# Batch 0 of a cross-attention and snake MLP kernel: x loaded flat, attention in token halves, and a new order of all steps

## The chip, the cores and the metric

One NeuronCore of one Trainium2 chip. The metric is device time in microseconds (us); of the kernel before there are three runs, 221.13, 221.16 and 221.43, median 221.16. All durations come from one profiled execution of 221.2 us. Engines: TensorE (PE; its weight loads PEld overlap the products), VectorE (DVE), ScalarE (ACT), GpSimd (POOL) and SyncE (SP, which only issues DMAs). "Landing" is when a DMA signals that its data is there.

## The reference

```python
B, H, S, Ns, D = 8, 8, 512, 32, 64          # x: [B,H,S,D], state: [B,H,Ns,D]
scores = x @ state.T / 8 ; a = softmax(scores)        # over 32 states
xread = a @ state                                     # [B,H,512,64]
scores2 = state @ x.T / 8 ; a2 = softmax(scores2)     # over 512 tokens
sread = a2 @ x                                        # [B,H,32,64]
y = concat([xread, sread], tokens) -> [B*544, H*D=512]
h = y @ w_in                                          # w_in 512 x 2048
s = sin(alpha * h) ; g = h + s*s / (alpha + 1e-9)
out = g @ w_out                                       # w_out 2048 x 512, out [4352, 512] float32
```

## The kernel before

All products are in bf16 with float32 sums in PSUM. `w_in` is folded into the state first: for each batch, `m(b, s)` computes M = state @ w_in for a quarter s of the 2048 columns (eight 64x32 products of 512 columns in both halves g of the heads, which run packed in the array), and `me` evicts it. Then h needs only the normalised attention A, transposed to AT: `h(t, f)` (or `hg`, one product per g) makes a tile of 128 columns of d_ff by 512 tokens with two products, M stationary, AT moving. There are 16 tiles f per batch. `si` applies Sin on ScalarE, `sq` squares it on VectorE (V), ScalarE (A) or GpSimd (G), `gt` adds h on VectorE and frees the PSUM bank of h. `o(t, st, f0, f1)` multiplies gT by w_out for one of four groups st of 128 tokens, 16 products of 512 columns in all; `oc` evicts it, `os` stores it from SP.

Attention of a batch: `sc` scores (128 tokens by 64 states of two heads, per product), `ex` Exp, `rs` row sums, `rr` reciprocals, `nm` normalises to A, then A is transposed: on TensorE for batch 0 (`at`, `ac` copies it out), by a DMA transpose from SP for the others (`ad`). x comes in as `xnat` (`lx`, a cast load from GpSimd, token rows p, each partition holding four tokens of every head), `pk` reorders it to `xp`, and it is transposed on TensorE for batches 0 and 1 and by a DMA transpose (`td`) from batch 2 on. The other side (sread) uses the same E: `w` = xp stationary times E, `cs` the column sums, `rc` and `xs` the division into `xs_all`; its MLP is tile row t = 8 with tiles of 256 columns.

Order: nothing is scheduled at run time. ORDER is a list of steps written out for the whole kernel, and each engine executes its own instructions in the order of that list; the trailing letter is the engine and the trailing digits are PSUM banks (there are eight, one tile each, so a step that takes a bank waits for the readers of what was in it). `warm_up.n.cols.bank` puts n spare products of zeros into a bank. Loads by GpSimd (`li` a quarter of w_in, `lo` a quarter of w_out, `l_st` the whole state, `lx` x of a batch) are carried out in the order in which they are issued; from the ninth on, an issue waits for the landing of the eighth before it.

Before, batch 0's x is loaded as float32 by four DMAs from SP (`lq`, L261, 256 KB each, rows of 1 KB), cast and reordered by ScalarE (`xq`, L356), transposed (`xtq`, L361) and copied out (`xc`, L385). The first two batches' state comes by `l_s01`, is transposed (`s01_t`) and put into `stT` block by block (`s01_k`). `touch_x` and `touch` are tiny first reads of x and w_in. The steps st_t and st_c turn the rest of the state round. The order of GpSimd's loads is st, li.0, li.1, li.2, lo.0, lo.1, lx.1, li.3, lo.2, then (after the two `nm` of batch 0) lo.3, lx.2.

Of the kernel before, what the change touches and what calls it, by code (L numbers as in the profile page):

```python
# [33 lines left out]
me.1.1.1.A warm_up.2.128.2 gt.0.2 si.0.0 warm_up.2.128.2 warm_up.2.128.6 warm_up.2.128.3
warm_up.2.128.2 warm_up.2.128.6 me.0.1.0.A gt.0.1 sq.0.0.G m.0.2.3.2 si.0.3 m.1.2.5.6 hg.0.4.0.7
me.0.2.0.V me.0.2.1.A hg.0.4.1 sq.0.3.G hg.0.6.0.4 me.1.2.1.V hg.0.6.1 si.0.4 hg.0.7.0.3 hg.0.11.0.2
me.1.2.0.V si.0.6 hg.0.7.1 sq.0.4.G hg.0.5.0.6 gt.0.0 hg.0.5.1 si.0.7 hg.0.11.1 hg.0.8.0.5 hg.0.8.1
sq.0.6.A gt.0.3 sq.0.7.G o.0.3.0.2.0 si.0.5 gt.0.4 o.0.3.2.3 o.0.0.0.2.1 si.0.11 o.0.0.2.3 gt.0.6
sq.0.5.G o.0.0.3.4 o.0.2.0.1.7 si.0.8 o.0.3.3.5 sq.0.11.A gt.0.7 hg.0.9.0.4 sq.0.8.G o.0.2.1.2
gt.0.5 o.0.2.2.4 hg.0.9.1 gt.0.11 o.0.0.4.5 hg.0.10.0.3 si.0.9 o.0.2.4.5 gt.0.8 o.0.0.5.6 o.0.3.5.6  # L40
sq.0.9.A o.0.3.6.8 pk.1.0.V hg.0.10.1 xt.1.1.6 pk.1.1.V si.0.10 gt.0.9 xt.1.0.2 xc.1.1.0.A sq.0.10.G
o.0.2.5.6 xc.1.1.1.V xc.1.0.0.A o.0.0.6.7 xc.1.0.1.V o.0.0.7.8 o.0.2.6.7 sc.1.1.5 gt.0.10 sc.1.0.4
m.0.3.6.2 ex.1.0 o.0.2.7.8 me.0.3.0.V o.0.1.0.3.3 me.0.3.1.V o.0.1.3.6 hg.0.13.0.6 o.0.1.6.7 ex.1.1
rs.1.0 hg.0.13.1 m.1.3.2.4 si.0.13 o.0.1.7.8 rr.1.0 rs.1.1 nm.1.0.0.4.G o.0.1.8.9 hg.0.12.0.5
o.0.3.8.9 rr.1.1 hg.0.12.1 me.1.3.0.V o.0.0.8.9 nm.1.1.0.4.G o.0.1.9.10 o.0.0.9.10 me.1.3.1.V
si.0.12 o.0.0.10.11 o.0.3.9.11 sq.0.13.G ad.1 hg.0.15.0.2 sq.0.12.A o.0.1.10.12 hg.0.15.1 gt.0.12
o.0.2.8.10 si.0.15 o.0.2.10.11 gt.0.13 o.0.0.11.12 hg.0.14.0.4 sq.0.15.A hg.0.14.1 o.0.3.11.13
si.0.14 gt.0.15 o.0.0.12.13 o.0.1.12.13 o.0.3.13.14 sq.0.14.A pk.2.0.V o.0.1.13.14 pk.2.1.V h.1.2.5
gt.0.14 h.1.4.6 td.2 si.1.2 lx.3.0.1 h.1.0.2 si.1.4 o.0.0.13.15 sq.1.2.V h.1.1.4 si.1.0 gt.1.2
sq.1.4.G o.0.3.14.16 si.1.1 o.0.2.11.13 sq.1.0.A oc.0.3.V h.1.6.5 sq.1.1.G gt.1.4 o.0.2.13.14 os.0.3  # L50
h.1.3.0 si.1.6 gt.1.0 o.0.1.14.16 si.1.3 sq.1.6.G h.1.13.6 gt.1.1 oc.0.1.A o.0.2.14.15 o.0.0.15.16
si.1.13 h.1.15.2 sq.1.3.G gt.1.6 os.0.1 o.0.2.15.16 oc.0.0.A h.1.5.4 sq.1.13.G oc.0.2.V si.1.15
h.1.7.3 os.0.0 gt.1.3 o.1.1.0.1.5 si.1.5 os.0.2 h.1.8.1 sq.1.15.G gt.1.13 o.1.1.1.2 si.1.7
o.1.2.0.2.7 sq.1.5.A o.1.1.2.3 sq.1.7.G h.1.12.0 gt.1.15 si.1.8 h.1.9.6 gt.1.5 o.1.2.2.3 si.1.12
sq.1.8.G o.1.2.3.5 gt.1.7 si.1.9 o.1.1.3.4 h.1.10.2 sq.1.12.A pk.3.1.V h.1.11.4 sq.1.9.G gt.1.8
o.1.2.5.6 si.1.10 o.1.2.6.7 gt.1.12 h.1.14.3 si.1.11 sq.1.10.G o.1.2.7.8 gt.1.9 sc.2.1.1 si.1.14
o.1.1.4.7 sq.1.11.A pk.3.0.V sq.1.14.G o.1.1.7.8 gt.1.10 td.3 o.1.2.8.9 sc.2.0.0 o.1.1.8.9 gt.1.11
o.1.1.9.10 ex.2.0 o.1.3.0.2.6 gt.1.14 o.1.3.2.4 o.1.2.9.10 o.1.3.4.5 o.1.2.10.12 ex.2.1 o.1.2.12.13
rs.2.0 o.1.1.10.11 m.2.2.2.4.3.0 rr.2.0 rs.2.1 o.1.2.13.14 nm.2.0.0.4.G me.2.3.0.A o.1.2.14.15 w.0.1
rr.2.1 me.2.2.1.A me.2.3.1.V o.1.3.5.6 nm.2.1.0.4.G me.2.2.0.A o.1.3.6.7 o.1.2.15.16 cs.0 oc.1.2.A  # L60
m.2.0.3.4.0.2 ad.2 rc.0 o.1.3.7.8 me.2.1.1.A o.1.3.8.9 sc.3.0.7 xs.0.1 me.2.1.0.A o.1.1.11.12 os.1.2
me.2.0.0.V sc.3.1.2 me.2.0.1.A o.1.1.12.13 o.1.3.9.10 xs.0.0 o.1.3.10.11 ex.3.0 o.1.1.13.16 ex.3.1
rs.3.0 o.1.3.11.13 oc.1.1.A o.1.3.13.14 rr.3.0 h.2.0.0 rs.3.1 nm.3.0.0.4.G os.1.1 o.1.3.14.16 si.2.0
rr.3.1 h.2.1.3 oc.1.3.V nm.3.1.0.4.G h.2.2.4 h.2.8.1 os.1.3 h.2.3.7 lx.4.0.1 ad.3 si.2.2 o.1.0.0.3.2
si.2.8 sq.2.0.V o.1.0.3.4 sq.2.2.G gt.2.0 h.2.4.5 si.2.1 o.1.0.4.6 si.2.3 sq.2.8.G o.1.0.6.7 gt.2.2
h.2.9.6 si.2.4 o.2.3.0.1.0 o.1.0.7.8 sq.2.1.G o.1.0.8.9 sq.2.3.A gt.2.8 o.1.0.9.10 h.2.5.4 si.2.9
gt.2.3 o.1.0.10.11 sq.2.4.G o.1.0.11.12 si.2.5 h.2.7.1 gt.2.1 o.1.0.12.13 sq.2.9.A sq.2.5.G
o.1.0.13.14 gt.2.4 o.1.0.14.15 si.2.7 o.1.0.15.16 o.2.0.0.1.7 gt.2.9 o.2.0.1.2 oc.1.0.A h.2.6.3
sq.2.7.G gt.2.5 o.2.3.1.2 os.1.0 o.2.3.2.3 si.2.6 h.2.10.5 pk.4.1.V pk.4.0.V o.2.3.3.4 sq.2.6.A
# [88 lines left out]
class Steps:  # L158
# [505 lines left out]
```

The softmax here doesn't subtract the row's maximum and nothing guards it: scores larger than these inputs give would overflow.

## Time and profile before

| Quantity | us or share |
|---|---|
| median of three runs | 221.16 |
| profiled execution, first to last instruction | 221.2 |
| TensorE busy (spare products among it) | 215.7 |
| ScalarE / VectorE / GpSimd busy | 173.5 / 162.4 / 107.1 |
| first h product | 15.11 |
| first o product | 22.55 |
| last landing of the queued start loads (lx.2) | 34.68 |
| last product ends / last store lands | 218.1 / 220.3 |

In the rows that follow a timeline line gives start and length in us, engine, line, operation, written tile <- read tiles, shapes, count, and in brackets the idle time before it and who ended it. A stage row gives the stretch, its length, and per engine the busy time and the number of instructions. A product of 512 columns is listed with some 0.38 us because its latency is counted; the next one starts 0.216 us later.

The landings of the start loads, by the DMA issues in narrow windows (issue, then landing): st_nat 3.25, 8.93; li.0 3.99, 11.58; li.1 4.74, 14.12; li.2 5.47, 16.72; lo.0 6.20, 19.20; lo.1 6.94, 21.74; lx.1 7.67, 24.40; li.3 8.55, 26.94; lo.2 9.29, 29.49; lo.3 14.23, 32.03; lx.2 15.04, 34.68.

### The profile page before, as it was taken

To read this page: it belongs to the slowest core of one execution; us is meant where nothing else is said; L and a number is where in the kernel's file an instruction comes from. 1 tells how busy PE (TensorE), PEld (TensorE's weight loads), DVE (VectorE), ACT (ScalarE), POOL (GpSimd) and SP (SyncE) were. 2 spreads that over 40 slices of the span, in tenths; PEclk is the share of its full clock that TensorE was granted. 3 is DMA by queue.
4 is the path that set the end of the run, shared out by engine and by line. 5 is a ranking of instruction groups with operands and counts; after the bars stand their busy time and mean duration, and the time that the engine had idled before them with its cause. 6 is when DMAs were issued, how large, how long until landed. Compare 5 with 4: busy or idle time off the path is not lost.

```text
span 221.2 us, 4330 instructions
## 1 busy us (share of the span) xinstructions
PE 215.7 (97%) x1619; PEld 106.0 (48%) x1619; DVE 162.4 (73%) x286; ACT 173.5 (78%) x297; POOL 107.1 (48%) x115
## 2 busy tenths in 40 slices
PE   7999999999999999999999999999999999999994
PEld 3664454444444444444454444445445555665452
DVE  3468986999678979988888778889766988571201
ACT  3589878998899979998996999798857897685111
POOL 6866626595388728934863377363501072121000
PEclk9999999999999999999999999999999999999999
DMA  6999995953549518375325437380220211012042
GB/s 172 198 206 204 205 203 87 174 199 73 119 127 158 96 50 150 44 190 61 81 41 125 126 95 94 108 117 17 47 99 0 98 47 47 0 50 95 1 142 96
DMA packets 38052, 23.48 MB, mean 106 GB/s; under 512 B 20992, under 2 KB 33680, under 8 KB 38032
## 3 DMA queue, kind: packets, MB, share of 16 engines
q0 software_dynamic: 11648, 8.13, 26.1%
q1 hardware_dynamic: 26128, 15.08, 26.1%
q8 instruction: 12, 0.20, 0.4%
q14 instruction: 8, 0.07, 0.1%
q10 hardware_dynamic: 256, 0.01, 0.1%
HBM read 17.44 MB, written 8.91 MB: 119 GB/s over the span
## 4 chain that ended last, share of the span: by engine, by line
PE 93%; ACT 3%; DMA 2%; SPq 0%; issue 0%
PE o_ps L587 54%; PE h_ps L537 22%; PE m_ps L488 4%; PE h_ps L543 3%; PE h_ps L552 3%; DMA x<-in_x_dram 2%; PE s_ps L399 2%; PE warm_ps L303 2%; PE w_ps L450 2%; PE w_ps L461 1%; PE x_ps L361 1%; ACT L226 1%; ACT s L560 1%; ACT M L496 1%; PE x_ps L376 0%; PE st_ps L333 0%
## 5 line engine op out<-in xcount | busy, mean ns | idle before, releaser
L587 PE MATMUL o_ps<-w_out_sb,gT 128*128 128x512 bf16 (+2 forms) x560 | 137.7, 373 | 0.0
L576 DVE SCALAR_TENSOR_TENSOR gT<-s,inva_sb,h_ps 128x512 bf16<-128x512 bf16 (+1 forms) x144 | 96.6, 714 | 18.8 <-POOL s L201 9.6
L201 POOL TENSOR_TENSOR s<-s 128x512 bf16<-128x512 bf16 (+1 forms) x76 | 76.7, 1021 | 65.9 <-ACT s L560 62.4
L560 ACT ACTIVATE s<-h_ps,alpha_sb 128x512 bf16<-128x512 f32 (+1 forms) x144 | 88.8, 671 | 10.5 <-PE h_ps L543 4.3
L587 PEld LDWEIGHTS <-gT 128*128 128x128 bf16 x560 | 52.3, 98 | 60.3 <-issue 5.0
L537 PE MATMUL h_ps<-AT,M 128*128 128x512 bf16 x224 | 60.8, 379 | 0.0
L537 PEld LDWEIGHTS <-M 128*128 128x128 bf16 x224 | 21.7, 98 | 25.9 <-issue 0.4
L569 ACT ACTIVATE s<-s 128x512 bf16<-128x512 bf16 (+1 forms) x53 | 31.4, 595 | 0.8
L201 POOL TENSOR_TENSOR A<-E,rR 128x512 bf16<-128x512 bf16 x16 | 16.6, 1048 | 25.7 <-ACT o_sb L595 12.7
L595 ACT COPY o_sb<-o_ps 128x512 f32<-128x512 f32 (+2 forms) x24 | 13.7, 571 | 16.6 <-PE o_ps L587 16.5
L496 ACT CAST M<-m_ps 128x512 bf16<-128x512 f32 x35 | 18.6, 594 | 8.2 <-PE m_ps L488 8.1
L496 DVE CAST M<-m_ps 128x512 bf16<-128x512 f32 x29 | 18.9, 679 | 2.5 <-PE m_ps L488 2.1
L595 DVE COPY o_sb<-o_ps 128x512 f32<-128x512 f32 x11 | 7.6, 691 | 13.0 <-PE o_ps L587 12.9
L303 PE MATMUL warm_ps<-warm 128*128 128x128 bf16 (+3 forms) x66 | 9.9, 295 | 1.4 <-DVE warm L209 1.2
L410 DVE TENSOR_REDUCE R<-E 128x16 f32<-128x512 bf16 x16 | 10.4, 658 | 1.1 <-ACT E L406 0.9
L201 DVE TENSOR_TENSOR s<-s 128x512 bf16<-128x512 bf16 (+1 forms) x15 | 6.2, 415 | 6.8 <-ACT s L560 6.7
L488 PE MATMUL m_ps<-w_in_sb,stT 64*32 64x512 bf16 x256 | 10.2, 382 | 0.0
L468 DVE RECIPROCAL rC<-w_ps 128x128 f32<-128x128 f32 x8 | 7.6, 948 | 3.2 <-PE w_ps L461 3.2
L406 ACT ACTIVATE E<-s_ps 128x512 bf16<-128x512 f32 x16 | 8.8, 601 | 1.4 <-PE s_ps L399 1.3
L552 PE MATMUL h_ps<-AT,M 128*128 128x512 bf16 x32 | 9.4, 380 | 0.4 <-ACT M L496 0.4
L543 PE MATMUL h_ps<-xs_all,w_in_sb 128*128 128x256 bf16 x64 | 9.1, 273 | 0.0
L560 ACT ACT_TABLE_LOAD x5 | 6.4, 1283 | 2.2 <-PE h_ps L537 1.1
(56 smaller groups left out, 104.3 us busy)
## 6 DMA issues: line engine op xcount, KB each, us to landing
out_dram<-o_sb SPq DMA_DIRECT2D x33, 256.0 KB, 2.3
xnat<-in_x_dram POOLq DMA_DIRECT2D x7, 512.0 KB, 7.7
w_in_sb<-in_moe_w_in_dram POOLq DMA_DIRECT2D x4, 512.0 KB, 10.3
w_out_sb<-in_moe_w_out_dram POOLq DMA_DIRECT2D x4, 512.0 KB, 16.3
x<-in_x_dram SPq DMA_DIRECT2D x4, 256.0 KB, 4.3
st_nat<-in_state_dram POOLq DMA_DIRECT2D x1, 256.0 KB, 5.7
out_dram<-o_sb SPq DMA_DIRECT2D x1, 192.0 KB, 1.9
s<-in_state_dram SPq DMA_DIRECT2D x1, 128.0 KB, 2.1
```

The costliest lines, as they stand in the source:

```text
L201: {"V": k.nc.vector, "G": k.nc.gpsimd}[eng].tensor_tensor(out, a, b, ALU.mult)
L303: k.nc.tensor.matmul(wp[:, :cols], k.warm[:, 0:k.P], k.warm[:, :cols], start=True, stop=True)
L488: k.nc.tensor.matmul(k.t["m", b, s + n, g][o0:o0 + k.Ns, :], k.stT[k.half(r), b * k.G + g, c0:c0 + k.Ns], k.w_in_sb[k.half(r), 2 * g + h, ...
L496: k.copy(eng)(k.t["M", b][:, g, s * k.FW:(s + 1) * k.FW], k.t["m", b, s, g][:])
L537: k.nc.tensor.matmul(hp[:, :n], k.t["M", t][:, g, fs], k.t["AT", t][:, g, :], start=(g == 0), stop=(g == k.G - 1),)
L543: k.nc.tensor.matmul(hp[:, :n], k.w_in_sb[:, q, fs], k.xs_all[:, q].rearrange("p b j -> p (b j)"), start=(q == 0), stop=(q == k.Q - 1),)
L552: k.nc.tensor.matmul(k.t["h", t, f][:], k.t["M", t][:, g, f * k.P:(f + 1) * k.P], k.t["AT", t][:, g, :], start=(g == 0), stop=(g == k.G - 1),)
L560: k.nc.scalar.activation(s[:, :n], k.t["h", t, f][:, :n], ACT.Sin, scale=k.alpha_sb[:, f:f + 1])
L569: k.nc.scalar.activation(s2[:, :n], s[:, :n], ACT.Square)
L576: k.nc.vector.scalar_tensor_tensor(gT[:, :n], k.t["s2", t, f][:, :n], k.inva_sb[:, f:f + 1], k.t["h", t, f][:, :n], ALU.mult, ALU.add,)
L587: k.nc.tensor.matmul(k.t["o", t, st, half][:, cols], k.t["gT", t, f][:, rows], k.w_out_sb[:, f, cols], start=(f == 0), stop=(f == k.FT - 1),)
L595: k.copy(eng)(o_sb[:, cols], k.t["o", t, st, half][:, cols])
```

## The change

Batch 0's x is read in the flat order of memory: partition = head x 16 + block of 32 tokens, and each partition holds 32 tokens in one run of 8 KB. Tokens 0-7 and 8-15 of every block come as float32 from SP (`lf`), tokens 16-31 by one cast load from GpSimd (`lfb`), which is its first. `xn` casts the first two parts; `xth` transposes four pairs of tokens per part on TensorE. A half e of the tokens is two parts, so scores, Exp, sums, reciprocals, `at0` and `ac0` go by halves, and `hh` makes half an h tile (two products of 256 columns). Scores are now one head per product (64 rows, 32 columns), two rows of the array in turn, against `st0T`, a second copy of the state. For `w.0` x in token order is needed: a DMA transpose `td.0` makes it from xT0, and `w` of batch 0 is 32 products of 32 columns. Stores of batch 0 write rows in the new token order.

The order is new up to the middle of batch 1: GpSimd's loads go lfb, li.0, li.1, lx.1, lo.0, li.2, lo.1, st, then (after two nm) li.3, lo.2, later lx.2, lo.3, lx.3; x of batch 1 is transposed before batch 0's o products begin; o runs one f at a time over all four token groups; `ad.1` and `td.2` follow in the list the issue of lo.3 and lx.3; spare products are of 256 to 512 columns. From the batches 2 on, only bank numbers differ, except `td.0` ahead of `td.3`.

```diff
-touch_x l_s01 consts touch lq.0.S ident_ l_alpha lq.1.S zero.0 warm_up.7.512.3 exp_table lq.2.S
-zero.1 identf.V lq.3.S s01_c.G l_st li.0 xq.0.A s01_t.4 li.1 xtq.0.5 warm_up.1.384.3 xq.1.A
...
+l_s01 ident_ touch_x consts lf.0.S touch zero.0 lfb lf.1.S l_alpha identf.V li.0 zero.1 exp_table
+li.1 s01_c.V warm_up.4.512.7 s01_t.0 lx.1.0.1 s01_0.A s01_k.1.V s01_k.0.A lo.0 xn.0.V
+warm_up.2.512.7 xth.0.0.1 li.2 xn.1.A xc.0.0.V lo.1 warm_up.1.512.0 warm_up.1.256.7 xth.0.1.2 l_st
+xth.0.2.3 xc.0.1.A xth.0.3.4 xc.0.2.A sc0.0.5.6 xc.0.3.V al_t.7 ex0.0.0 sc0.1.0.1 al_c ex0.0.1 inva
+ex0.1.0 rs0.0 ex0.1.1 rs0.1 rr0.0 warm_up.1.480.5 m.0.0.2.3 rr0.1 m.1.0.4.7 nm.0.0.0.2.V
+nm.0.1.0.2.G me.0.0.0.A nm.0.0.2.4.V me.0.0.1.A nm.0.1.2.4.G warm_up.5.512.1 at0.0.5 me.1.0.1.V
+m.0.1.6.0 sin_table li.3 at0.1.1 ac0.0.V m.1.1.2.3 ac0.1.V lo.2 hh.0.0.0.7 me.0.1.1.V hh.0.1.0.5
+hh.0.2.0.1 me.0.1.0.A hh.0.0.1 me.1.0.0.V hh.0.1.1 me.1.1.0.A hh.0.3.0.0 hh.0.4.0.6 me.1.1.1.V
+hh.0.2.1 si.0.0 hh.0.5.0.4 hh.0.3.1 pk.1.0.V si.0.1 hh.0.4.1 pk.1.1.V sq.0.0.G hh.0.5.1 si.0.2
+sq.0.1.V si.0.3 xt.1.1.2 gt.0.1 sq.0.2.G si.0.4 xt.1.0.3 gt.0.0 hh.0.6.0.5 xc.1.1.0.A sq.0.3.G
+gt.0.2 hh.0.6.1 xc.1.1.1.A hh.0.7.0.7 hh.0.7.1 xc.1.0.0.V xc.1.0.1.A o.0.0.0.1.1 sq.0.4.G gt.0.3
+sc.1.1.2 si.0.5 o.0.0.1.2 sc.1.0.3 o.0.0.2.3 ex.1.1 o.0.1.0.1.0 sq.0.5.V o.0.1.1.2 gt.0.4 o.0.1.2.3
...
+me.0.2.1.V o.0.2.4.5 o.0.3.4.5 si.0.7 st_t.0.4 rr.1.0 sq.0.6.G rr.1.1 st_t.1.3 sq.0.7.A st_c.0.0.V
+o.0.0.5.6 nm.1.0.0.4.G st_c.0.1.A gt.0.6 o.0.1.5.6 st_c.1.0.A o.0.2.5.6 hh.0.8.0.4 gt.0.7 st_c.1.1.A
...
 def touch_x(k):
-        k.touched_x = k.const.tile([16, k.H], FP32, name="touched_x")
...
+        k.touched_x = k.const.tile([16, 1], FP32, name="touched_x")
+        k.nc.scalar.dma_start(k.touched_x[:].unsqueeze(2), k.flat()[::8, 0:1, 0:1])
-    def lq(k, q, eng):
...
+    def flat(k):
+        return k.x[0].rearrange("h (b j) d -> (h b) j d", j=32)
+    def lf(k, part, eng):
+        k.t["xa", part] = k.const.tile([k.P, 8, k.D], FP32, name=f"xa_{part}")
         {"A": k.nc.scalar, "S": k.nc.sync}[eng].dma_start(
+            k.t["xa", part][:], k.flat()[:, 8 * part:8 * part + 8, :]
+        )
+    def lfb(k):
+        k.nc.gpsimd.dma_start(k.flat_sb()[:, 16:32, :], k.flat()[:, 16:32, :])
+    def xn(k, part, eng):
+        k.copy(eng)(k.flat_sb()[:, 8 * part:8 * part + 8, :], k.t["xa", part][:])
+    def xth(k, b, part, bank):
+        tp = k.t["xth", b, part] = k.ps(bank, [k.P, 4, k.P], BF16, "x_ps")
+        for m in range(4):
+            j = 8 * part + 2 * m
+            k.nc.tensor.transpose(
+                tp[:, m, :], k.flat_sb()[:, j:j + 2, :].rearrange("p j d -> p (j d)"), k.ident[:]
+            )
+    def td(k, b):
+        if b == 0:
+            xp = k.new(0, "xp", k.xppool, [k.P, 2, k.H, 2, k.D], BF16)
+            k.nc.sync.dma_start_transpose(
+                xp[:].rearrange("p e h r d -> p (e h) (r d)"),
+                k.xT0()[:].rearrange("p e h m t -> p (e h m t)"),
+            )
+            return
+    def sc0(k, half, *banks):
+        for r in range(2):
+            sp = k.t["sc0", half, r] = k.ps(banks[r], [k.P, k.H, k.Ns], FP32, "s_ps")
+        for h in range(k.H):
+            for r in range(2):
+                k.nc.tensor.matmul(
+                    k.t["sc0", half, r][:, h, :],
+                    k.xT0()[k.half(r), half, h].rearrange("d m t -> d (m t)"),
+                    k.st0T[k.half(r), h, :],
+                    start=True, stop=True,
+                )
+    def at0(k, half, bank):
+        tp = k.t["at0", half] = k.ps(bank, [k.P, k.G, 2, k.P], BF16, "a_ps")
+        for i in range(2):
+            for g in range(k.G):
+                k.nc.tensor.transpose(tp[:, g, i, :], k.t["A", 0][:, g, 2 * half + i], k.ident[:])
+    def hh(k, t, f, half, *bank):
+        if bank:
+            k.t["h", t, f] = k.ps(bank[0], [k.P, k.S], FP32, "h_ps")
+        c = slice(256 * half, 256 * half + 256)
+        for g in range(k.G):
+            k.nc.tensor.matmul(
+                k.t["h", t, f][:, c], k.t["M", t][:, g, f * k.P:(f + 1) * k.P],
+                k.t["AT", t][:, g, c], start=(g == 0), stop=(g == k.G - 1),
+            )
     def w(k, b, bank):
+        if b == 0:
+            for h in range(k.H):
+                for i in range(k.C):
+                    r, c = h % 2, h % 4 * k.Ns
+                    k.nc.tensor.matmul(
+                        wc[k.half(r), h // 2, r * k.Ns:(r + 1) * k.Ns],
+                        k.t["xp", 0][:, i // 2, h, i % 2, :], E[:, h // 4, i, c:c + k.Ns],
+                        start=(i == 0), stop=(i == k.C - 1),
+                    )
+            return
     def os(k, t, st, half=None):
+        if t == 0:
+            ov = k.out[0:k.S].rearrange("(b e m r) c -> e r m b c", b=16, e=2, m=8)
+            k.nc.sync.dma_start(ov[st // 2, st % 2][:, :, cols], o_sb[:, cols])
```

The functions ex0, rs0, rr0 and ac0 are the old ones on half of the tokens; xc of batch 0 copies a transposed part into xT0; s01_0 copies the transposed state into st0T.

## The prediction

> **What bounds the kernel now.** I read the page first, then TensorE's busy time by stage, its timeline over the first 24 us, and the landing of each load in narrow windows.
>
> ```profile
> PE 215.7 (97%) x1619; PEld 106.0 (48%) x1619; DVE 162.4 (73%) x286; ACT 173.5 (78%) x297; POOL 107.1 (48%) x115
> ...
> PE   7999999999999999999999999999999999999994
> ...
> DMA  6999995953549518375325437380220211012042
> ```
> TensorE is full in all slices but the first and the last; the DMA engines are full only in the first six (33 us). Busy time by stage (columns TensorE, weight loads, VectorE, ScalarE, GpSimd, clock, DMA share, GB/s):
>
> ```profile
> 0.00:10.40 10.40, 8.60 (x52) 4.68 (x53) 3.78 (x13) 5.27 (x9) 7.88 (x16) 1.00 0.85 184
> 10.40:20.00 9.60, 8.95 (x155) 5.66 (x154) 6.90 (x15) 8.06 (x15) 5.28 (x6) 1.00 1.24 206
> 20.00:24.00 4.00, 4.00 (x19) 1.82 (x20) 4.00 (x7) 4.00 (x8) 3.78 (x5) 1.00 1.38 200
> ...
> 36.00:218.10 182.10, 182.10 (x1291) 87.96 (x1289) 137.82 (x236) 146.07 (x252) 84.10 (x85) 1.00 0.42 90
> ```
> From 20.0 on TensorE never waits: 197.9 us of products, the last at 217.88, and 3.3 us of output behind it. What it does before 20.0 is in its timeline:
>
> ```profile
> 1.19 3.17 PE L303 MATMUL warm_ps<-warm 128*128 128x512 bf16 x7 [1.19 <-DVE warm L209]
> ...
> 9.74 1.08 PE L303 MATMUL warm_ps<-warm 128*128 128x128 bf16 x10
> ...
> 15.11 0.39 PE L552 MATMUL h_ps<-AT,M 128*128 128x512 bf16 x1
> 15.89 1.24 PE L552 MATMUL h_ps<-AT,M 128*128 128x512 bf16 x5 [0.39 <-ACT M L496]
> ...
> 19.95 2.76 PE L552 MATMUL h_ps<-AT,M 128*128 128x512 bf16 x12
> 22.55 2.32 PE L587 MATMUL o_ps<-w_out_sb,gT 128*128 128x512 bf16 x10
> ```
> "Busy" there is largely spare products. Useful: 48 transposes, 16 scores, six groups of m, 9 of 32 h products, 8 transposes of A: some 6.3 us at full clock. So 13.7 of 20 us are lost, and only these can be won. Spare products of 512 columns start every 427 ns, of 128 columns every 55 ns after 10.4: the clock doubles at 10.4.
>
> **What the skill says.** "TensorE: Matmul & The Clock Gate", Part 1, has the array at half rate until it was busy for one free-running window of about 3.4 us; the doubling at 10.4 agrees. Its Part 4 says that transposes don't count as busy in the same way; no row here shows it. "TensorEngine Tiling (Array Packing)", Key Properties: a change of tiling mode drains TensorE. This agrees: an o product before or after an m group takes 309 ns to the next start instead of 216, so one m group alone costs 0.42 us. "DMA: Bandwidth & Descriptors", Queues, rings and completion order: each DMA engine goes round its queues, so a transpose from SP does not stand behind GpSimd's loads, it shares with them. Issued alone, and together with a transpose, a load of x lands after
>
> ```profile
> xnat<-in_x_dram POOLq DMA_DIRECT2D x1, 512.0 KB, 5.9
> ```
> ```profile
> xnat<-in_x_dram POOLq DMA_DIRECT2D x1, 512.0 KB, 7.7
> ```
>
> **The change, part by part.** *Loads.* Half of x now goes through GpSimd as its first load (lfb), with the shape of st_nat (4 KB read, 2 KB written per partition), which took 5.7 us. GpSimd is free at 1.31, so 7.0 (6.3 without the loads beside it, 7.6 if they slow it more). Behind st_nat (landed 8.93) the next load came 2.65 later, then one each 2.54. Hence li.0 9.65 (before 11.58), li.1 12.2 (14.12), lx.1 14.85 (24.40), lo.0 17.4 (19.20), li.2 19.9 (16.72), lo.1 22.5 (21.74), st 23.8 (8.93), li.3 26.3, lo.2 28.85, lx.2 31.5, lo.3 34.05 (before: last one 34.68). li.3 and lo.2 now stand behind two nm on GpSimd (issued about 12.4), lx.2 and lo.3 behind four squares (about 19.5): the queue has work until 23.8, so this costs nothing.
>
> *Attention.* s01 lands at 2.86 as before. VectorE casts it (estimate 0.3, from 0.2 to 0.4: no such row), then 8 transposes 0.64, copies 0.36 (ScalarE), 0.43 (VectorE), 0.36 (ScalarE) in turn, cast xn.1 0.62: 5.8. Four groups xth at 0.43 (half clock), the last two held by lfb: 7.07 to 7.93. Scores: 32 instead of 16; the score rows take 29 ns warm, 53 cold, I take 40: to 9.3. Four Exp at 0.36 (the 64x256 copy's time) spaced 0.3: 10.2. Two sums 0.68 and two reciprocals 0.25 on VectorE: 11.45; half of nm 0.33 (estimate from 256 elements of a 512-element sum) and 0.55 on GpSimd (half of 1.05): 11.9. TensorE meanwhile does two m and five spare products (1.1). at0 0.22; VectorE first evicts an m (0.68), then copies AT: **first h product at 13.05**, before 15.11 and then a wait.
>
> New waits, and what stands behind them: on TensorE m.0.1 (needs li.1, 12.2) stands ahead of at0.1 (needs A's second half, 12.4), so a li.1 later than 12.4 holds the second half of every h tile; on VectorE pk.1 (needs lx.1, 14.85) comes up at 15.15, and the square and every gt of batch 0 stand behind it; in before these waited for nothing, since x of batch 1 was read only at 26.9. xn.1 on ScalarE stands behind the state copies, and xth.0.1 behind xn.1. The table loads (1.28 each) are as many as before and the first Sin one comes at 11.8 instead of 13.7.
>
> *VectorE then sets the pace*: ac0.1 0.35, three evictions 0.62, two pk 0.34, a square 0.4, gt.0.1 0.74: 17.1. TensorE has 12 half tiles of h, two products each, 0.218 per half tile (2.62) and the transposes of batch 1 (1.1), at 16.8 it waits for that gt, then for gt.0.0 and gt.0.2 (0.67 each): first o at 18.45 (before 22.55).
>
> *To 36 us.* 48 o at 0.216 (10.35), 8 h (3.49), scores of batch 1 (0.5), st_t (1.1), three single m (1.27) make 16.7; waits 0.95: for xc.1.0.1 on ScalarE (0.3), gt.0.4 (0.2), Exp behind its table load (0.1), the four st_c in a row (0.3). So 36.1. Loads come in time: lo.1 22.5 for 23.4, st 23.8 for 24.3, lo.2 28.85 for 30.05, lo.3 34.05 for 36.1. From there gT and evictions lead the products; I allow 0.1.
>
> *Sum.* Of the 197.9 us that before needs after 20.0, the changed kernel has done by 36.1: 48 o 10.35, 23 h products 4.96, xt 1.1, scores 0.5, one m 0.42, together 17.35. Left 180.5. w.0 becomes 32 products of 32 columns: the trace has 16 at 32 ns (0.51); the skill's floor of 25 ns ("The Clock Gate", Part 1) and this row give 30 ns, 0.96, so +0.5 with the mode change (0 if the two column halves run together, 1.3 if 64-column weights take 55 ns). 36.1 + 180.5 + 0.5 + 0.1 = 217.2 against 217.88: **-0.65 us**. The profiled 221.19 stands 0.03 over the median 221.16, so **220.5**.
>
> *At nothing:* td.0, on SP in front of td.3: 1.75 to 3.2 of issue at about 48, td.3 was issued at 52.2; lands by about 53 and w.0 is at 57. Uncovered, scores of batch 3 would wait. Stores of batch 0 in 8x16 rows: six o_sb buffers hide them. touch_x with 16 elements, moved constants: ScalarE waits for its table anyway.
>
> **The rivals.** *The clock opens late (slower).* In the window that ended at 10.4 the old kernel had 1.75 us of wide spare products; the changed one has 0.4, small scores and transposes, and earlier it stands about 0.7 us at 4.5 waiting for xn.0, 0.3 for lfb. If the window doesn't count as busy, the next ends at 13.8: the five spare products take 2.13 instead of 1.08, at0 ends 13.2, everything behind VectorE comes 1.3 later: 221.8. It decides if TensorE idles over about 0.5 us between 7.0 and 10.4, say li.0 after 10.2. For it: Part 4 and the narrow work; against it: the stretch is filled end to end.
>
> *The lead is lost in the loads (no change).* ad.1 leaves when nm.1.1 ends, now about 27.5 with lo.2, lx.2 and lo.3 still coming (before: 35.02, after the last landing 34.68). It costs a load 1.8 us by the rows above; lo.2 then lands at up to 30.6, lo.3 at 35.9: stalls of 0.6 to 1: 221.1 to 221.5. For it: the margins are 0.5 to 0.9; against: a transpose's own packets are 1.4 us.
>
> *It doesn't do what it says:* half-length h products and the bigger w.0 eat the lead; 1.3 for w.0 gives 221.3.
>
> *More is won:* VectorE's estimates too long, lfb at 6.3: 0.7 to 1.3 earlier, 219.2 to 219.8.
>
> **How the numbers follow.** My ledger 0.45 (219.9 to 220.9; 220.5), late clock 0.22 (221.3 to 222.3), loads 0.13, lead eaten 0.09, more won 0.11. A measurement of this kernel can tell about 0.2% (0.44 us). Faster: 0.11 plus 0.37 of the ledger's 0.45; same: 0.08 of it, 0.06 of loads, 0.06 of eaten; the rest slower. The range leaves 0.1 on each side: 219.2 to 222.2; the ledger's own is 219.9 to 220.9.
>
> **What would show it.** Right: h products start near 13, o near 18.5, TensorE without gaps over 0.3 us after 26, last product near 217.2, scores of 32 columns at 30 to 40 ns. Wrong: spare products still 427 ns apart after 11 (clock); gaps in front of o that end on a w_out load, or a transpose landing over 5 us after issue (loads); w.0 over 1.2 us; lfb after 7.6, which shifts the whole start.

## The result, and the profile after

The changed kernel takes 230.53 us (229.26 to 231.59 in four runs) against 221.21 for the kernel before: a ratio of 1.0406, 95% interval 1.0364 to 1.0447. I had forecast 220.5, faster by 0.3%. The page of one execution of the changed kernel (time 231.59, span 229.6):

```profile
PE 217.3 (95%) x1631; PEld 106.2 (46%) x1631; DVE 167.4 (73%) x291; ACT 173.9 (76%) x299; POOL 104.1 (45%) x112
...
PE   5895999998999979999999999999999999999994
...
PEclk9678899999999999999999999999999999999999
DMA  5999999517837841917715431761040200111042
```

TensorE now has holes in three places where it had none: in slices 1 to 4 (0 to 23 us), of which 2 to 4 also have a clock below 9; in slice 10 (52 to 57 us); and in slice 15 (80 to 86 us). The stages of the start, same columns and stretches as before:

```profile
0.00:10.40 10.40, 7.00 (x74) 3.32 (x82) 4.45 (x15) 5.33 (x11) 6.73 (x14) 0.88 0.86 161
10.40:20.00 9.60, 8.63 (x101) 4.92 (x86) 8.06 (x15) 7.43 (x13) 5.84 (x7) 0.78 1.31 205
20.00:24.00 4.00, 2.33 (x14) 1.53 (x14) 3.80 (x6) 0.97 (x3) 3.30 (x4) 0.69 1.20 206
```

From 20 to 24, where the old kernel was full at full clock (4.00, 1.00), TensorE is busy for 2.33 us at a clock of 0.69 and ScalarE for 0.97, while VectorE works nearly throughout (3.80). TensorE's timeline there, then VectorE's and GpSimd's:

```profile
11.21 2.31 PE L310 MATMUL warm_ps<-warm 128*128 128x512 bf16 x5
...
15.22 2.79 PE L480 MATMUL h_ps<-AT,M 128*128 128x256 bf16 x24
17.95 1.08 PE L385 MATMUL x_ps<-ident,xnat 128*64 128x128 bf16 x32
21.66 1.86 PE L480 MATMUL h_ps<-AT,M 128*128 128x256 bf16 x8 [2.64 <-DVE gT L677]
23.32 0.63 PE L688 MATMUL o_ps<-w_out_sb,gT 128*128 128x512 bf16 x1
```

```profile
17.12 2.45 DVE L355 COPY xp<-xnat 128x1024 bf16<-128x1024 bf16 x2
19.49 1.25 DVE L201 TENSOR_TENSOR s<-s 128x512 bf16<-128x512 bf16 x1
20.86 2.07 DVE L677 SCALAR_TENSOR_TENSOR gT<-s,inva_sb,h_ps 128x512 bf16<-128x512 bf16 x3
```

```profile
17.08 4.57 POOL L201 TENSOR_TENSOR s<-s 128x512 bf16<-128x512 bf16 x4 [2.68 <-ACT s L661]
```

The two pk copies of batch 1 took 1.27 and 1.26 us, the square 1.25. In the same trace the same copies took 0.42 at 38.4 and the same square 0.42 at 24.5. What differs is the last row: GpSimd ran four squares end to end beside them. TensorE waited 2.64 us for the gT behind them.

But a GpSimd square alongside is not enough. In the kernel before, pk.3.1 started inside a row of nine GpSimd squares and still took 0.42 us (GpSimd's square of that moment, then the copy):

```profile
48.45 1.04 POOL L201 TENSOR_TENSOR s<-s 128x512 bf16<-128x512 bf16 x1
49.41 0.42 DVE L348 COPY xp<-xnat 128x1024 bf16<-128x1024 bf16 x1
```

It started 0.08 us before that square ended. In the changed kernel the first copy started 0.05 us after a square of 1.04 us had begun, and the second copy and VectorE's square 0.09 and 0.24 us after the two that followed. One sum fits all three: what was left of the GpSimd square (0.99, 0.98 and 0.98 us) plus 0.28. It fits, to within 0.01 us, every such copy and square in the fifteen profiles that started with more than 0.15 us of a GpSimd product still to run; with less left they took their own 0.42. So the price depends on when VectorE comes, and each of these three had come just after a GpSimd square had started.

The third hole is one wait for the DMA transpose of batch 4's x, which landed 5.9 us after its issue instead of 4.3:

```profile
85.31 0.64 PE L490 MATMUL s_ps<-stT,xT 128*128 128x64 bf16 x16 [1.71 <-DMA xT<-xp]
```

**Three intervals that can be compared.** TensorE's work from the first h product to the first o, from there to the column sums of batch 0 (cs.0), and from there to the last product is the same in all versions of the changed kernel; the third is the same in the kernel before too. Starts of products, in us, from one profile each; the time is the median of four runs (for the second profile of the kernel before, that one execution). The runs of one version lie up to 2.4 us apart, so a difference between two versions whose runs overlap shows little by itself, and the profiled execution can be any of the four: what a change does is read from the intervals.

| Kernel | first h starts | to first o | to cs.0 | to last product | time |
|---|---|---|---|---|---|
| before, first profile | 15.11 | 7.44 | 34.92 | 160.41 | 221.2 |
| before, second profile | 14.02 | 6.66 | 34.92 | 160.43 | 221.2 |
| after | 15.22 | 8.10 | 40.61 | 162.30 | 230.5 |
| pk.1 later | 16.84 | 5.40 | 40.44 | 162.13 | 229.0 |
| two squares to ScalarE | 15.19 | 5.37 | 40.70 | 164.73 | 231.6 |
| start filled | 13.85 | 7.90 | 40.92 | 161.23 | 229.4 |
| pk.1 and pk.3 later | 13.94 | 5.40 | 39.93 | 162.43 | 227.4 |
| the same, narrow spare products | 15.73 | 5.40 | 39.95 | 160.47 | 226.8 |
| the same, batch 4's x early | 16.54 | 5.40 | 39.94 | 160.41 | 227.1 |
| that, start filled | 14.07 | 5.40 | 39.93 | 160.41 | 225.2 |
| that, no contended squares | 14.00 | 5.60 | 39.99 | 160.41 | 225.3 |
| two squares to ScalarE, batch 4's x early | 15.98 | 5.38 | 40.71 | 160.41 | 226.6 |
| after, batch 4's x early | 15.25 | 8.11 | 40.62 | 160.41 | 229.0 |
| squares of VectorE left out | 13.80 | 4.88 | 38.94 | 160.41 | 224.4 |
| squares of GpSimd left out | 13.72 | 5.04 | 39.02 | 160.52 | 223.7 |

### The profile page after: what moved, and what is told of

Read it like the earlier page. It is cut to its first block, busy times and chain, and to the rows that moved or that the text cites. A ratio compares the mean times of both kernels' runs of the same rounds, so it can differ in the third digit from the quotient of the medians.

```text
span 229.6 us, 4360 instructions
## 1 busy us (share of the span) xinstructions
PE 217.3 (95%) x1631; PEld 106.2 (46%) x1631; DVE 167.4 (73%) x291; ACT 173.9 (76%) x299; POOL 104.1 (45%) x112
## 4 chain that ended last, share of the span: by engine, by line
PE 77%; DMA 6%; issue 5%; DVE 5%; POOL 4%; ACT 1%; POOLq 0%; DVEq 0%
PE o_ps L688 45%; PE h_ps L638 18%; PE m_ps L589 4%; DMA w_in_sb<-in_moe_w_in_dram 3%; PE h_ps L644 3%; POOL s L201 3%; DMA xT<-xp 3%; PE s_ps L490 2%; DVE xp L355 2%; DVE gT L677 2%; PE w_ps L551 1%; PE h_ps L480 1%; PE w_ps L562 1%; PE warm_ps L310 1%; DVE M L597 1%
## 5 line engine op out<-in xcount | busy, mean ns | idle before, releaser
L201 POOL TENSOR_TENSOR s<-s 128x512 bf16<-128x512 bf16 (+1 forms) x73 | 73.9, 1026 | 77.3 <-ACT s L661 76.0
L638 PE MATMUL h_ps<-AT,M 128*128 128x512 bf16 x204 | 55.5, 379 | 0.2 <-DVE gT L677 0.2
L638 PEld LDWEIGHTS <-M 128*128 128x128 bf16 x204 | 19.8, 98 | 23.9 <-issue 0.9
L670 ACT ACTIVATE s<-s 128x512 bf16<-128x512 bf16 (+1 forms) x50 | 29.4, 590 | 0.8
L201 POOL TENSOR_TENSOR A<-E,rR 128x512 bf16<-128x512 bf16 (+1 forms) x16 | 16.0, 1014 | 27.1 <-ACT o_sb L696 14.5
L597 DVE CAST M<-m_ps 128x512 bf16<-128x512 f32 x26 | 16.9, 678 | 3.2 <-PE m_ps L589 3.1
L201 DVE TENSOR_TENSOR s<-s 128x512 bf16<-128x512 bf16 (+1 forms) x21 | 10.3, 492 | 8.9 <-ACT s L661 8.6
L589 PE MATMUL m_ps<-w_in_sb,stT 64*32 64x512 bf16 x256 | 11.9, 404 | 0.1
L480 PE MATMUL h_ps<-AT,M 128*128 128x256 bf16 x64 | 8.6, 290 | 2.8 <-DVE gT L677 2.6
L355 DVE COPY xp<-xnat 128x1024 bf16<-128x1024 bf16 x14 | 8.1, 612 | 1.1 <-DMA xnat<-in_x_dram 1.1
L480 PEld LDWEIGHTS <-M 128*128 128x128 bf16 x64 | 6.5, 102 | 4.7 <-issue 3.4
## 6 DMA issues: line engine op xcount, KB each, us to landing
w_out_sb<-in_moe_w_out_dram POOLq DMA_DIRECT2D x4, 512.0 KB, 15.2
```

The source lines that it names most:

```text
L201: {"V": k.nc.vector, "G": k.nc.gpsimd}[eng].tensor_tensor(out, a, b, ALU.mult)
L355: k.copy(eng)(k.t["xp", b][:, :, hs, :], k.t["xnat", b][:, hs, :].rearrange("p h (i d) -> p i h d", i=k.C),)
L480: k.nc.tensor.matmul(k.t["h", t, f][:, c], k.t["M", t][:, g, f * k.P:(f + 1) * k.P], k.t["AT", t][:, g, c], start=(g == 0), stop=(g == k.G ...
L589: k.nc.tensor.matmul(k.t["m", b, s + n, g][o0:o0 + k.Ns, :], k.stT[k.half(r), b * k.G + g, c0:c0 + k.Ns], k.w_in_sb[k.half(r), 2 * g + h, ...
L597: k.copy(eng)(k.t["M", b][:, g, s * k.FW:(s + 1) * k.FW], k.t["m", b, s, g][:])
L638: k.nc.tensor.matmul(hp[:, :n], k.t["M", t][:, g, fs], k.t["AT", t][:, g, :], start=(g == 0), stop=(g == k.G - 1),)
```

## The experiments

**pk of batch 1 moved on VectorE.** It is needed only for w.1.

```diff
-hh.0.3.1 pk.1.0.V si.0.1 hh.0.4.1 pk.1.1.V sq.0.0.G
+hh.0.3.1 si.0.1 hh.0.4.1 sq.0.0.G
...
-o.0.1.3.4 gt.0.5 o.0.2.0.1.6
+o.0.1.3.4 gt.0.5 pk.1.0.V pk.1.1.V o.0.2.0.1.6
```

> The changed kernel with the two pk of batch 1 moved on VectorE from ahead of the first square to behind gt.0.5, where GpSimd has no squares. Theory A (VectorE and GpSimd slow each other: the two copies took 1.27 and 1.26 us beside four GpSimd squares, 0.42 elsewhere, and the square and every gt stand behind them): the two copies return to 0.42 each, TensorE's 2.64 us of waiting ahead of the ninth pair of half products shrinks to under 0.6, first o at about 21 instead of 23.3, and the time falls by 2 to 4 us, to 226 to 228.5. Theory B (VectorE was late because lx.1 landed late and would be late anyway): the wait shrinks by under 1 us, time 229 to 230.5. Theory C (the lead is lost in the half clock, which comes from the narrow work before 8): the wait shrinks, but the time stays at 229 to 230.

229.00 us, 1.5 less than after. VectorE, then TensorE, of this run:

```profile
19.23 0.79 DVE L201 TENSOR_TENSOR s<-s 128x512 bf16<-128x512 bf16 x1 [0.40 <-ACT s L661]
...
25.43 0.75 DVE L355 COPY xp<-xnat 128x1024 bf16<-128x1024 bf16 x2
```

```profile
20.93 1.26 PE L480 MATMUL h_ps<-AT,M 128*128 128x256 bf16 x8 [0.27 <-DVE gT L677]
```

The pair of copies is back at 0.75 us, the wait fell from 2.64 to 0.27, and the first interval from 8.10 to 5.40. The time missed theory A's 226 to 228.5, and 1.5 us is within the scatter of the runs (228.51 to 230.18, against 229.26 to 231.59): this execution's first h started only at 16.84, since lf.1 landed late (the cast behind it began at 8.24 instead of 6.47) and the clock opened only at 16.35 (below). So theory A has the interval; in the time it is not seen.

**Two squares of GpSimd on ScalarE, pk left where it is.** This parts contention from pk's place in the order.

```diff
-pk.1.1.V sq.0.0.G hh.0.5.1
+sq.0.0.A hh.0.4.1 pk.1.1.V hh.0.5.1
...
-si.0.3 xt.1.1.2 gt.0.1 sq.0.2.G si.0.4
+si.0.3 sq.0.2.A xt.1.1.2 gt.0.1 si.0.4
```

> The changed kernel with the squares sq.0.0 and sq.0.2 on ScalarE instead of GpSimd; the two pk of batch 1 stay where they are. Theory A (contention of VectorE with GpSimd): with GpSimd idle from 17 to 19 the pk take 0.42 us each instead of 1.27, the square sq.0.1 about 0.43 instead of 1.26, first o at about 21, time lower by 1.5 to 3.5 us, 227 to 229. If it is only the place of pk in VectorE's order (its own 0.42 each and lx.1's landing), the pk still take about 1.27 and nothing moves: 229 to 231.5.

```profile
17.08 0.75 DVE L355 COPY xp<-xnat 128x1024 bf16<-128x1024 bf16 x2
17.75 0.42 DVE L201 TENSOR_TENSOR s<-s 128x512 bf16<-128x512 bf16 x1
```

Same place, same start as in the changed kernel (17.08 and 17.12), but GpSimd idle: 0.75 instead of 2.45, and the first interval is 5.37. So it is the contention and not the place. The time, however, stayed at 231.57, where theory A had 227 to 229. The gain went later:

```profile
79.78 0.59 PE L638 MATMUL h_ps<-AT,M 128*128 128x512 bf16 x2 [2.29 <-DVE gT L677]
...
85.08 0.64 PE L490 MATMUL s_ps<-stT,xT 128*128 128x64 bf16 x16 [1.68 <-DMA xT<-xp]
```

The load of batch 4's x took 9.9 us here (8.3 in the changed kernel; why it was longer is not shown); VectorE stood at pk.4 with every gt behind it, and then the transpose took 5.9.

**The same with batch 4's x loaded early** (the edit is that of the run named "batch 4's x early" below).

> The kernel with sq.0.0 and sq.0.2 on ScalarE, which gained 2.7 us up to 61 and lost all of it at 77 to 85, now with batch 4's x loaded behind batch 3's, its pk and its transpose ahead of the first squares of batch 2. If the gain was lost only because batch 4's x came late (load 9.9 us, transpose 5.9 us): no wait over 0.5 us between 70 and 90, 227 to 228 instead of 231.6. If something else took it, 229 or more.

226.59 us, 5.0 below and a little better than the 227 to 228 expected; from cs.0 on 160.41 as in the kernel before. The two squares on ScalarE did gain; the late x had taken it.

**TensorE's early waits filled with spare products.**

```diff
-xn.0.V warm_up.2.512.7 xth.0.0.1
+xn.0.V warm_up.7.512.7 xth.0.0.1
...
-warm_up.1.512.0 warm_up.1.256.7 xth.0.1.2
+warm_up.3.512.0 warm_up.1.256.7 xth.0.1.2
```

> The changed kernel with seven instead of two spare products of 512 columns ahead of the first transposes of x and three instead of one ahead of the second ones, so that TensorE's waits of 1.16 and 0.49 us before 7.2 are filled. Theory C (the clock falls back to half between 7.9 and 14.7 since TensorE idled before): full clock from about 4.5 on, the five spare products ahead of at0 take 1.1 instead of 2.3 us, first h product at about 14 instead of 15.2, time lower by 1 to 2 us. Theory A: first h product may come 1 us sooner, but the pk then start no sooner than lx.1 lands (16.3), so the time falls by under 1 us, 229 to 230.5.

The first h is at 13.85, 1.4 us sooner: theory C's size. The time of 229.38, 1.15 less, can't part C from A (the runs, 229.12 to 230.02, overlap the changed kernel's). In the changed kernel the trace has the clock full from 4.5 to 7.9, half to 14.7, full, and half again from 21.5 to 25, after the 2.64 us wait; the five spare products took 2.31. In this run it is full from 7.0 to 20.6, and half again for 3.4 us behind the same wait. In all five profiles with the filled start the clock opens between 6.1 and 7.4 and stays open up to the first h, which comes at 13.72 to 14.07. In the eight without, three open at 4.5 to 4.9 and fall back at 7.9 to 8.3, and five open only at 9.5 to 16.4; their first h is at 13.94 to 16.84 (the two latest, 16.84 and 16.54, also had lf.1 land 1.8 us late). In time it shows further down, where the same filling takes 1.9 us off with ranges that don't touch. The seven products cover TensorE's 1.16 us wait for xn.0; that this wait is what keeps the clock back is the reading that fits, but it was not parted from the sheer amount of work that the fill adds.

**pk.3.1 moved next to pk.3.0**, on top of pk.1's move.

```diff
-sq.1.12.A pk.3.1.V h.1.11.3
+sq.1.12.A h.1.11.3
...
-sq.1.11.A pk.3.0.V sq.1.14.G
+sq.1.11.A pk.3.1.V pk.3.0.V sq.1.14.G
```

> As the run with the pk of batch 1 moved, and pk.3.1 also moved on VectorE from 55.3 (1.26 us beside seven GpSimd squares, TensorE waited 0.75 us behind it ahead of the first scores of batch 2) to just ahead of pk.3.0, after those squares. Theory A: another 0.6 to 1 us lower than that run, and the wait ahead of the scores of batch 2 gone. Rival: the wait belongs to the squares on GpSimd that gt needs, not to pk: under 0.3 us of difference.

227.40, another 1.6, where theory A had 0.6 to 1. The wait of 0.75 us ahead of the scores of batch 2 is gone, but a contended copy remained (53.07, 1.26 us beside GpSimd's last square), so the interval to cs.0 fell by 0.5 only. More than that is not pk.3.1's: the first h of this profile came at 13.94 instead of 16.84, without anything in its edit that could move it.

**Narrow spare products: the same time, 20 products more.**

```diff
-warm_up.2.512.7
+warm_up.7.128.7
...
-warm_up.5.512.1
+warm_up.20.128.1
```

> The kernel with the pk of batches 1 and 3 moved, and in it 7 of the spare products of 512 columns cut into 27 of 128 or fewer in the same time (20 of 128 for 5, and 7 of 128 for 2), nothing else. Theory D (a 16 KB transfer of TensorE's instructions, about every 125 products, runs on one DMA engine for 0.95 us at 78.74, between the last packets of the DMA transpose of batch 4's x at 78.5 and that engine's share of its signal at 79.7, so the transpose lands 1.1 us late and the scores of batch 4 wait about 2.0 us): 20 more products ahead of it bring that transfer some 4 us sooner, before the transpose's packets; the transpose lands about 4.3 us after its issue instead of 6.0, the wait shrinks to about 0.6, and the time falls by 1.0 to 1.6 us, to 225.8 to 226.4. Theory E (the transpose is late only because batch 4's x was loaded late): landing still 5.9 us after issue, time 227 to 227.8.

The DMA rows between issue and landing of batch 4's transpose, of the run before this edit and of this one (queue: packets, MB, share; then the transpose with its time to landing):

```profile
q1 hardware_dynamic: 2080, 0.52, 42.7%
q8 instruction: 1, 0.02, 0.9%
...
xT<-xp SPq DMA_TRANSPOSE x1, 6.0
```

```profile
q1 hardware_dynamic: 2089, 0.54, 56.3%
...
xT<-xp SPq DMA_TRANSPOSE x1, 4.3
```

Such a 16 KB packet on the instruction queue comes about every 125 products of TensorE (91 to 153 in the changed kernel) and takes 0.9 to 1.6 us. The Trainium skill, "Runtime: NRT & Kernel Launch", section Instruction fetch mechanics, has instructions fetched in 16 KiB blocks of 256, a cost "mostly hidden". Size and spacing agree (a product is a weight load and a matmul); what was not hidden here is what the packet did to another transfer. In the changed kernel the data packets of td.4 end and the instruction packet starts at 83.25, it lasts 0.93, and the last two 4-byte packets of the transpose come at 84.17 and 84.18. A landing is sixteen updates of one semaphore: fifteen came from 83.56 to 83.71, the sixteenth at 85.27, and TensorE started at 85.31. The packet accounts for 0.9 us of this; why the last update came 1.1 us behind its packet, where the others took some 0.5, is not shown. In this run the instruction packet came at 75.0, before the transpose, all sixteen updates came from 80.43 to 80.59, and the transpose landed in 4.3 us: cs.0 to last product 160.47 instead of 162.43. Theory D holds for the landing, and it is chance: the position follows from how many products came before. In time the gain was 0.6 at the median, less than the 1.0 to 1.6 expected and within the scatter (225.02 to 227.43), since the clock was at half from 8.3 to 15.2 in this profile (first h at 15.73).

**Batch 4's x loaded behind batch 3's.**

```diff
-lx.3.0.1
+lx.3.0.1 lx.4.0.1
...
-h.2.3.2 lx.4.0.1 ad.3 si.2.2 o.1.0.0.3.0 si.2.8 sq.2.0.V
+h.2.3.2 ad.3 si.2.2 o.1.0.0.3.0 si.2.8 pk.4.1.V pk.4.0.V td.4 sq.2.0.V
...
-si.2.6 h.2.10.6 pk.4.1.V pk.4.0.V o.2.3.3.4
+si.2.6 h.2.10.6 o.2.3.3.4
...
-h.2.11.0 td.4
+h.2.11.0
```

> The kernel with the pk of batches 1 and 3 moved, and batch 4's x loaded right behind batch 3's (about 31.6 instead of 65.5), its pk ahead of the first square of batch 2 and its DMA transpose right behind. Then the scores of batch 4 cannot wait for that transpose, whatever makes it late. Both D and E: the wait of 2.0 us at 78.6 goes, 225 to 226. If the load then disturbs the transposes ad.1 and td.2, waits of over 0.5 us appear at 39 or 52 and the time stays at 226.5 or more.

The tail is 160.41, 2.0 less than with both pk moved alone; ad.1 and td.2 landed in time. The time of 227.1 missed the 225 to 226: its first h started at 16.54, the second-latest start of all: lf.1 was late here too (its cast began at 8.28), and the clock opened at 15.6.

**The same edit alone, on the changed kernel.**

> The changed kernel with that one edit alone: batch 4's x loaded behind batch 3's, pk.4 and td.4 early. Theory D (td.4 lands late behind the transfer of instructions, 2.1 us of wait at 83): 228 to 228.8, about 2 us below the changed kernel's 230.5. If the wait at 83 only moves to the next transposes: 230 to 231.

228.99, 1.5 below the changed kernel, somewhat less than expected and with runs that overlap its own (228.08 to 229.78). The two profiles are the clean comparison: the starts of h and o and cs.0 repeat the changed kernel's to within 0.06 us, and the tail alone is shorter, by 1.89.

**Batch 4's x early and the start filled.**

> As the run with batch 4's x loaded early, and with the seven and three spare products ahead of the first transposes of x. Theory C (clock): full clock before 8 in every run, first h product at 13.3 instead of 13.9, time 0.4 to 1.0 us lower than that run. Rival: after the pk have left, first h waits for li.1 and VectorE's evictions, not for TensorE: within 0.3 us of that run.

225.23 (225.02 to 225.58, against 226.45 to 228.31), 1.9 below, more than theory C's 0.4 to 1.0, and the best of the versions that compute everything. The first h came at 14.07, not 13.3: with the clock open, the loads decide:

```profile
10.51 0.63 PE L589 MATMUL m_ps<-w_in_sb,stT 64*32 64x512 bf16 x16 [0.62 <-DMA w_in_sb<-in_moe_w_in_dram]
...
13.05 0.41 PE L589 MATMUL m_ps<-w_in_sb,stT 64*32 64x512 bf16 x8 [0.51 <-DMA w_in_sb<-in_moe_w_in_dram]
```

**The remaining contended squares on ScalarE, pk.3 behind GpSimd's last square.**

```diff
-sq.0.1.V
+sq.0.1.A
...
-sq.0.10.V
+sq.0.10.A
...
-sq.1.1.V
+sq.1.1.A
...
-sq.1.11.A pk.3.1.V pk.3.0.V sq.1.14.G o.1.1.7.8 gt.1.10 td.3 o.1.2.8.9
+sq.1.11.A sq.1.14.G o.1.1.7.8 gt.1.10 o.1.2.8.9
...
-gt.1.11 o.1.1.9.10
+gt.1.11 pk.3.1.V pk.3.0.V td.3 o.1.1.9.10
```

> As the run with batch 4's x loaded early and the start filled with spare products (225.2), and the three squares that VectorE did beside GpSimd's squares (sq.0.1, sq.0.10, sq.1.1, 0.79 us each instead of 0.42) go to ScalarE (0.63), and both pk.3 with the DMA transpose go behind gt.1.11, after GpSimd's last square. Theory A (what TensorE still loses between 20 and 56, 3.4 us against 0.5 in the kernel before, is the rest of the contention): the waits for gT at 18.2, 42.5 and 55.5 (0.3, 0.2 and 0.3 us) go, 224.2 to 224.8. Theory F (it is the order of o one tile at a time over four token groups, with no gT in store, and the single m): the squares on ScalarE delay the next Sin by as much, 225 to 226.

225.33: nothing. The wait at 56 went, those at 18 and 43 grew from 0.3 to 0.5 and from 0.2 to 0.5. Theory A does not explain what is left.

**Squares left out.** In two versions gT of batches 0 and 1 is made from s where VectorE (8 tiles) or GpSimd (17 tiles) made the square.

```diff
 def sq(k, t, f, eng):
+    if t < 2 and eng == "V":
+        k.t["s2", t, f] = k.t["s", t, f]
+        return
```

> As the run with batch 4's x loaded early and the start filled (225.2), but the eight squares of batches 0 and 1 that VectorE makes are left out (gT is made from s instead of s squared there), so VectorE has some 4.5 us less to do between 16 and 47, and GpSimd's squares no partner to contend with. Theory G (the nine small waits of TensorE between 20 and 56, 2.3 us together, are for a VectorE that has too much to do): at least five of the waits go, 223 to 224. Theory F (they come from the order: o follows each gT at once and only four banks are left for h): the waits stay within 0.6 us in sum, 224.6 to 225.4.

> The same with the seventeen squares of GpSimd in batches 0 and 1 left out instead (gT from s there). Theory H (the waits come through the time of a GpSimd square, 1.04 us, between a Sin and its gT, and through what it costs VectorE): the waits at 18.2, 20.4, 42.5, 47.2, 48.5 and 55.5 go, 1.5 to 2.5 us less, 222.7 to 223.8. Theory F: under 0.6 us less.

224.38 and 223.71: 0.85 and 1.5 less. The first (223.66 to 225.24) overlaps the filled version and lies in neither theory's range. The second (223.53 to 224.12) is clear of it and meets H's range at its upper edge. Of the nine waits that the filled version shows between 18 and 59 us, six go in the first, as G had it, and eight in the second; one new wait comes in each. In the profiles the two save 0.5 and 0.4 before the first o, and 1.0 and 0.9 from there to cs.0. What does that leave? As an estimate I took what TensorE's products of o, h, m, scores and transposes cost at their full rate from the time that passed. Between first o and cs.0 the kernel before loses 0.7 us, the filled version 4.25, these two 3.25 and 3.35. So some 2.6 us of this remain with the squares of one engine gone: in the first version two waits for gT of 0.3, in both the m groups of one quarter (0.37 each around the products), a wait for stT of 0.2, and w.0. That these belong to the order itself (four o banks open from the first f, four left for h and m) is argued, not shown.

**The kernel before again.**

> The kernel before, unchanged, for a second profile: the first profile's span of 221.2 is as long as the median time, while all other runs have a time of 1.9 to 2.0 us over their span. If that first execution was a slow one, this one has a span of about 219.2, and the difference lies before 20 us, in the clock that opened at 10.4 or in waits for the loads of batch 0; if not, the span is 221.2 again.

Its span is 219.3 with a time of 221.24. Two rows of its timeline, to be held against 9.74 (ten products in 1.08) and 22.55 in the first profile:

```profile
10.14 1.62 PE L303 MATMUL warm_ps<-warm 128*128 128x128 bf16 x26
...
20.68 2.32 PE L587 MATMUL o_ps<-w_out_sb,gT 128*128 128x512 bf16 x10
```

The clock opened at 4.15 instead of 10.5, and the first o came 1.87 us sooner; from there on the two profiles are alike to 0.02 us. "TensorE: Matmul & The Clock Gate", Part 1, calls the window free-running and the ramp "run-variable"; two executions of one kernel agree. It calls its cost under 1% of a typical span; here the two differ by 0.8%, which is four times the 0.2% that a measurement of this kernel can tell.

## Why the prediction was wrong

The profiled execution (231.59, the slowest of the four) is 11.1 us over my 220.5. By the intervals: 2.0 of the baseline, 2.2 up to the first h, 2.7 to the first o, 1.9 behind cs.0, and the 2.3 that remain between first o and cs.0.

- **The baseline, 2.0 us: the step "the profiled 221.19 stands 0.03 over the median".** 221.19 was a span. In the runs of the kernel before that state both, the time is 1.85 to 1.94 us more than the span (up to 2.1 in the versions that compute everything, up to 2.5 with VectorE's squares left out), so that execution was some 2 us slower than the median ones. My sum against it gave a span of 220.5, so a time of 222.4: slower, by its own working, before anything else failed. The early hint was in the view that I used: the spare products ahead of 10.4 at half rate, beside a clock column that reads 1.00 there, since the trace's first clock record is only at 10.5.
- **VectorE's chain, 2.7 us: the step "two pk 0.34, a square 0.4".** I took the rate of back-to-back copies from rows where GpSimd was idle, and put the pk next to GpSimd's squares without asking; waiting for GpSimd stood in the sum at nothing. They cost 2.45 and 1.25, which took TensorE's wait from 0.27 to 2.64; another 0.35 of the 2.7 is the half clock that followed that wait. This is the term that failed. The rest of the interval was right: I had 18.45 minus 13.05, 5.40, and with the pk in its place but GpSimd idle it is 5.37. That the five versions with pk.1 moved have exactly 5.40 is in part luck, since there the pk are out of the chain and the square still costs 0.79. The skill has it in "SBUF — State Buffer", section Who interferes with whom: VectorE's copies in a two-port mode, and its products with both inputs in SBUF, share ports with GpSimd, and whoever issues first holds them for its whole instruction. The traces agree with the class (gT and the evictions, which read PSUM, kept their 0.63 to 0.75 us beside GpSimd squares) and with the order: VectorE paid the rest of the square that was running, plus 0.28. In the kernel before the same pair stood side by side for pk.3, and its timing hid it.
- **Up to the first h, 2.2 us.** lf.1 landed at 6.45 where my ledger needs it by about 5, xn.1 ended at 7.1 instead of 5.8, and li.0 and li.1 landed 0.5 late (10.18, 12.72). With the clock open this makes 13.72 to 14.07 instead of 13.05; the rest is the clock, as the rival *the clock opens late* had it: five spare products 2.31 (it said 2.13), at0 begun at 13.32 (it had it ended at 13.2). Its point of decision, idling between 7.0 and 10.4, was wrong by place: TensorE idled 1.16 and 0.49 us before 7.2. The rival also missed that the clock can fall a second time behind a long wait.
- **First o to cs.0, 2.3 us: the steps "waits 0.95" and "gT and evictions lead; I allow 0.1".** 0.5 of it is pk.3.1 beside seven GpSimd squares (this interval is 40.44 with pk.1 moved, 39.93 with pk.3.1 moved as well), the same failing as in the chain. The other 1.8 is only in part explained: the filled version still has four waits for gT of 0.17 to 0.34, 0.97 in all, and leaving out one engine's squares takes 0.9 to 1.0 off the interval. What makes up the rest is open.
- **Behind cs.0, 1.9 us: "from the batches 2 on, only bank numbers differ".** The order was the same and the time was not: the instruction transfer fell on td.4. No step of mine could have priced it; that td.4 had only 0.14 us to spare in the old kernel (landed 76.83, scores at 76.97) was readable.
- **w.0, overpriced:** it costs 0.27 more, not 0.5. From the o before to the o behind it are 0.95 us (0.68 before); its 32 products start 17 ns apart, where I had 30, since they come in pairs on two column halves, the case that I had in brackets.
- **Right:** twelve half tiles of h took from 15.22 to 17.95, 2.73 us, where I had 2.62. No wait for w_out, the state or ad.1: the rival *lead lost in the loads* did not happen. td.0 held SP for 5.6 us, not 1.75 to 3.2, and still td.3 was held by pk.3.0 (ended 58.83) and not by SP (free at 58.04).

Among the slower rivals only the clock, at 221.8, stood clear of the kernel's own scatter. No rival was "an engine beside another slows it".

## To carry to other kernels

When a change brings a VectorE copy, or a VectorE product of two SBUF inputs, next to a run of GpSimd instructions, price it as 0.28 us plus what is left of the GpSimd instruction that is running when it starts, up to a whole one, and ask what stands behind it on VectorE. That a profile shows it at its own duration beside GpSimd may be timing: look at what was left. Before summing against a profile, hold its span against the span of the timed runs: the profiled execution can itself be the odd one, and at the start the TensorE clock is the first thing to look at. A transfer that makes it with a few tenths of a microsecond to spare can become a wait when only the count of instructions changes; issue it earlier when nothing forbids it.

## What was not expected of the hardware

- A VectorE copy of 128x1024 bf16 took 0.42 us alone and 1.26 us beside back-to-back GpSimd squares of 1.04; a VectorE square 0.42 alone, 0.79 and 1.25 beside them. Each of these is 0.28 us plus what was left of the running GpSimd square (0.98, 0.51, 0.98). A copy that started first took its 0.42 to 0.43, and the GpSimd square that started during it up to 1.29.
- The clock fell back to half for 3.4 us after TensorE had waited 2.6 us, in the profiles of all three kernels that have this wait (after, the start filled, batch 4's x early alone); a wait of 2.29 us in another left it full. It may not fall each time: all four runs of the second kernel have a mean granted clock of 0.992 or 0.993, which is one such fall in 229 us, but of the eight runs of the other two, four have 0.999 or 1.000. The first h product moved by 2.9 us between two versions that differ only behind it (16.84 with pk.1 moved, 13.94 with both); 1.8 of it is where lf.1 landed.
- An instruction transfer of 16 KB held one DMA engine 0.93 us, and with it the completion of a DMA transpose: 5.9 to 6.0 us to landing in four kernels, 5.3 where the transfer fell among the transpose's own packets (start filled), 4.2 to 4.3 where it fell outside them.
- td.0, a DMA transpose of the same size as the others, took 5.5 to 6.0 us of SP to issue, where td.3 took 2.0 to 2.2. But td.2 took 4.0 to 6.3 in nine versions, too, so it need not be td.0's layout; what makes an issue long was not tried.
